# 56 small products of a constant first in TensorE's program, one summing loop for keys and values in every batch, and a new written order

## The chip, the cores and the metric

The kernel runs on one core of a Trainium2 chip. The metric is the device time of one execution in microseconds. It is measured in several runs; the comparison goes by the median. Besides, one execution is recorded by the hardware profiler, and all rows quoted here come from that one. Engines are named as the profile names them: PE (TensorE matmul), PEld (TensorE weight load), DVE (VectorE), ACT (ScalarE), POOL (GpSimd) and SP (SyncE, whose queue issues all the transfers here).

## What is computed

Attention over 32 memories per head, and behind it a feed-forward block with a spatial gate. There are 8 batches, 8 heads, 576 rows and 64 numbers per head; w_in has 512 x 1024 numbers.

```python
def _attn_ref(q, k, v, phi):
    a = phi - np.max(phi, axis=2, keepdims=True)
    a = np.exp(a)
    a = a / (np.sum(a, axis=2, keepdims=True) + 1e-09)
    k_m = np.einsum('bhsm,bhsd->bhmd', a, k)
    v_m = np.einsum('bhsm,bhsd->bhmd', a, v)
    scores = np.matmul(q, k_m.transpose(0, 1, 3, 2)) / np.sqrt(q.shape[-1])
    scores = scores - np.max(scores, axis=-1, keepdims=True)
    attn = np.exp(scores)
    attn = attn / (np.sum(attn, axis=-1, keepdims=True) + 1e-09)
    return np.matmul(attn, v_m)

def _moe_ref(x, w_in, w_spatial, b_spatial, w_out):
    h = np.maximum(x @ w_in, 0.0)
    u, v = h[..., :d_ff // 2], h[..., d_ff // 2:]
    v_n = (v - mean(v)) / np.sqrt(var(v) + 1e-06)
    v_s = np.einsum('ts,bsd->btd', w_spatial, v_n) + b_spatial[None, :, None]
    return (u * v_s) @ w_out
```

## The kernel before

Everything of a batch stays in the core's memory between loading and storing. The steps of one batch, with the letter that the written order uses for each and the names that the profile shows:

- P, `memory_weights`: load phi, take the largest value per memory over all rows (mx on VectorE; a transpose mt, a reduction cm, a broadcast cmb and a transpose back mb across the 128 partitions), subtract, exponentiate in place, and sum over rows (es).
- K, `memories`: load k and v into kv_sb, then sum phi-weighted rows with many small products of 64 partitions and 32 columns. In batches 1 to 7 one loop of 72 products takes k and v together (kvm, 128 columns wide, L411) and 8 more give the denominators (L422). Batch 0 goes another way, `first_memories`: 72 products for the keys (km, L334), the denominators (L349), scaling (den, kmn) and two transposes (tk, L373), and only later 72 products for the values (vm), vmn and tv.
- Q, `queries`: load q; batch 0 is transposed by TensorE (tq, L478, L489, L490) and copied by ScalarE (qT, L480, L494).
- S, `scores`: q times the key memories (sc). For batch 0, `first_scores` uses 64 + 16 small products (L531, L542), a softmax on VectorE and ScalarE (L560 to L579), transposes (at, L586) and the split into a high and a low part (ah, al).
- M, `products`: value memories times w_in (mp, L683), split into mh and ml. V, `gate`: pv, relu, normalisation, vh and vl. U, `units`: pu, relu, u. G, `spatial`: ps (L838), g, gh and gl. O, `project`: po (L878) and the store.

Every large product is made of three on parts of less precision (high x high, high x low, low x high).

The weights have steps of their own: D loads w_in in four pieces of 1 MB, E and L decode them (E the half that the gate uses, L the other), each in four operations: ScalarE scales (L174), GpSimd multiplies (L176), VectorE merges twice (L180, L184, the last into win_sb). W loads w_spatial, T transposes it (wt, L244; high part wth, L255; low part wtl), X does w_out, B the bias. Z is a filler: one product of the identity with itself that nobody reads (L897).

A low part can be made in two ways (`low`): VectorE subtracts, or TensorE adds minus the high part to the sum (L140) and ScalarE copies the rest (L149). The names in ON_VECTOR choose.

The order is written out by hand, in three tables: START, then PLAN once for each of batches 1 to 5, then END. A token such as S or K' runs the next part of that step, up to its next `yield`; primes mean batches ahead. Every engine works strictly through its own instructions in the order in which the tokens issue them, and SP issues transfers in that order too. A transfer into a buffer that is still being read waits on SP, with everything behind it. PSUM holds four single banks (`bank`) and two pairs (`banks`), which go round.

Of the kernel before, what the change touches and what calls it, by code (L numbers as in the profile page):

```python
# [10 lines left out]
F32 = mybir.dt.float32  # L11
# [26 lines left out]
    S' S G3 G1 G3 G0 G3 K'' G0 G1 K'' G0 G3 G0 K'' G1 S' G2*2 S'*2 O0 G2 G1 S' G3 G2 S' G3 K'''
    G1 Q'' G2 O1 G2 G3*2 S'*2 G2 S' M1' O2 P''' G3 S' O3 S' O2 S' O2 S' O0 O3 G2 V1' P''' U3' O0
    V1' P''' O4 G2 O0 O4 V0' S' K'' O3 O1 P''' O3 Q'' K'' O4 V4' O0 V0' U1' O1 V1' V0' O2 O1 M1  # L40
    V4' O4 O1 P'''
# [3 lines left out]
    U3 V1 V4 V0 K' U3 Q'*2 V4 V1 V3 V1 V4 U1 V4 U1 U2*2 V0*2 U0 U2 K' V0 V2 V4 Q' U0 V1 V3 V2  # L45
    M0' U0 M1' V3 S' V2 V4*2 V2 M0'*3 G0 M1' G0 M0' M1' V3 V2 M1'*2 V2*2 G1 G0 V3 G1 S' V3*2 G1
    S' V4 G1 G0 S'*3 G1 S' G3 G1 G3 G1 G3 G0 S'*2 U3 G0 S' G1 G2 S'*3 G1 G2 G0 S' G2 S' G0 G3 G2
    O0 S'*3 O3 S' G2 G0 V0' G2 V0' U3' V1' V0' V3' S' G3 G2 V1' V3' U2' G3 V3' G3*2 V0' V3' U2'
    O2 V4' U3' O0 U1' V0' U3' V0' U2' O0 U1' V1'*3 V4' V0' U0' V3' U0' V4'*2 O2 V4' U1' G0' U0'
    V1' G2 V4' V2' G3 V4' O1 G2 V1' V2' V4' G1' V2' V4' O2 V4' O1 G0' V3' V2' O2 V3' V2'*2 G1'  # L50
    V2' O0 O3 G0'*3 G1'*3 G3' G1' G3' G0' G2' G1' G0' G2'*2 O3 G3' G0'*2 G3' O3 G2' O3' G3'
    G1'*2 O1' G3' K' G3' O1 G2'*2 O0' O1 G2' G3' O0' O1' O3' O1' O3' O1' G2' O0' O2' O4' G3' O3'
    G2' O4'*2 O2' O0' O2' O4' O2' V0
# [9 lines left out]
def memory_attention_spatial_gate(  # L63
# [40 lines left out]

    ident = const.tile([P, P], F32, name="ident")
# [15 lines left out]
    nc.gpsimd.memset(t2[SR:P, :].bitcast(F32), 1.0)  # L121
# [151 lines left out]
    def over_rows(b, eng, to, op):  # L273
        if b == 0:
            nc.vector.tensor_reduce(to, phi_sb.rearrange("p j i m -> p j m i"), axis=AX.X, op=op)
# [3 lines left out]
        eng.tensor_tensor(half, phi_sb[:, :, 0:4], phi_sb[:, :, 4:8], op=op)
# [5 lines left out]
        eng.tensor_tensor(to, to, phi_sb[:, :, 8], op=op)  # L285
        yield

    def memory_weights(b, _):
# [7 lines left out]
        yield from over_rows(b, nc.vector, mx, ALU.max)  # L296
# [27 lines left out]
        yield from over_rows(b, engine(f"es{b}"), es, ALU.add)  # L324

    def first_memories():

        halves = (slice(0, 64), slice(64, P))

        def sums(n, to):  # L330
            for i in range(NX):
                for j in range(NJ):
                    for r in range(2):
                        nc.tensor.matmul(  # L334
                            to[r][32 * j : 32 * j + 32, 0:D],
                            phi_sb[halves[r], j, i, :],
                            kv_sb[halves[r], j, n, i * D : (i + 1) * D],
                            start=(i == 0),
                            stop=(i == NX - 1),
                        )  # L340

        km = [bank(f"km_{r}") for r in range(2)]
        sums(0, km)
        yield
        es = state.pop(("es", 0))
        esm = [x[:, D : D + 2] for x in km]
        for j in range(NJ):
            for r in range(2):
# [621 lines left out]
```

## Time and profile before

| what | value |
|---|---|
| time, median of 3 runs | 428.44 us (427.9 to 428.46) |
| the profiled execution's own time | 427.97 us |
| its span in the profile | 425.8 us |
| mean granted TensorE clock | 0.983 |
| PE busy | 404.0 us, 95% |
| DVE / ACT / POOL busy | 277.7 / 229.5 / 100.6 us |
| PE idle after 60 us, the largest groups | 3.2 us by "issue" in kvm, 2.4 us for ml |

How to read it: a row of the timeline gives start, duration, engine, source line, operation, output and inputs, partitions x elements and count; in brackets stands the idle time before it and what ended it. "Issue" means that nothing in the profile ended it. A row of the windows gives the stretch, its length and PE's busy time with the count of its products; where all engines are shown PEld, DVE, ACT and POOL follow likewise. Then come the granted TensorE clock as a share of full speed, the DMA engines' busy share, and GB/s. In a row of groups the busy time and the mean duration in ns follow the count, then the idle time before them. A row of the DMA view ends in KB and the us from issue to landing.

### The profile page before, as it was taken

Reading aid. Unit: us, or ns where it says so; the run is one execution under the profiler, and the core shown is the slowest. Engines: PE = TensorE matmul, PEld = TensorE weight load, DVE = VectorE, ACT = ScalarE, POOL = GpSimd, SP = SyncE. Lnnn points to the kernel's source line nnn. Section 1 sums busy time; section 2 is a strip of 40 time slices with the busy share of each in tenths; the row PEclk is TensorE's granted clock in tenths of the full one; section 3 lists DMA queues with packets and bytes.
Section 4 is the critical chain, followed back from the end, with each engine's and each line's share of the span. In section 5 each row is a group of like instructions: output and inputs, shape, how many; then the busy total and the mean of one; then the engine's idle time right before and its main releaser. Section 6 shows DMA issues by size and latency. Waiting matters only on the chain.

```text
span 425.8 us, 9900 instructions
## 1 busy us (share of the span) xinstructions
PE 404.0 (95%) x4179; PEld 348.8 (82%) x4179; DVE 277.7 (65%) x494; ACT 229.5 (54%) x444; POOL 100.6 (24%) x189
## 2 busy tenths in 40 slices
PE   6699899998999999999899999999999998999996
PEld 6486689786789887988698888988898877988984
DVE  3259557997888467884778377875787268944320
ACT  2438996546844287336843386337833384348312
POOL 1372574203300134012600134013401111132000
PEclk9859999999999999999999999999999999999999
DMA  8967927917580155705480157405700210000103
GB/s 308 386 267 186 241 66 225 215 37 262 138 221 3 53 183 115 167 0 181 92 219 2 74 162 184 97 26 185 112 4 0 75 50 2 0 2 25 45 32 123
DMA packets 85728, 50.73 MB, mean 119 GB/s; under 512 B 66162, under 2 KB 70258, under 8 KB 85684
## 3 DMA queue, kind: packets, MB, share of 16 engines
q1 hardware_dynamic: 85684, 50.10, 41.4%
q8 instruction: 33, 0.54, 0.6%
q14 instruction: 11, 0.09, 0.1%
HBM read 40.65 MB, written 9.44 MB: 118 GB/s over the span
## 4 chain that ended last, share of the span: by engine, by line
PE 76%; ACT 10%; DVE 7%; issue 3%; DMA 2%; POOL 1%; DVEq 0%; ACTq 0%; POOLq 0%
PE ps L838 24%; PE po L878 23%; PE pu L800 9%; PE pv L716 8%; PE kvm L411 2%; DVE ml L151 2%; PE mp L683 2%; ACT mh L692 1%; PE sc L616 1%; DMA phi_sb<-in_phi_dram 1%; PE sc L531 1%; PE wt L244 1%; ACT phi_sb L321 1%; DMA raw_out<-in_moe_w_out_dram 1%; ACT raw L174 1%
## 5 line engine op out<-in xcount | busy, mean ns | idle before, releaser
L860 ACT CAST gh<-g 128x512 fp32r<-128x512 f32 x32 | 19.8, 621 | 74.1 <-DVE g L849 74.1
L838 PE MATMUL ps<-wth,vh 128*128 128x288 f32 x256 | 56.5, 302 | 2.7 <-DVE ml L151 2.4
L838 PE MATMUL ps<-wth,vl 128*128 128x288 f32 x256 | 55.0, 296 | 0.0
L838 PE MATMUL ps<-wtl,vh 128*128 128x288 f32 x256 | 54.9, 296 | 0.0
L878 PE MATMUL po<-woh,gh 128*128 128x512 f32 x128 | 51.0, 398 | 0.0
L878 PE MATMUL po<-woh,gl 128*128 128x512 f32 x128 | 50.8, 397 | 0.0
L878 PE MATMUL po<-wol,gh 128*128 128x512 f32 x128 | 50.5, 394 | 0.0
L838 PEld LDWEIGHTS ps<-wth,vh 128*128 128x128 f32 x256 | 41.3, 188 | 6.4 <-issue 3.0
L761 DVE BATCH_NORM_STATS2 st<-vr 128x6 f32<-128x512 f32 (+1 forms) x35 | 23.8, 680 | 33.6 <-ACT vr L758 32.9
L838 PEld LDWEIGHTS ps<-wth,vl 128*128 128x128 f32 x256 | 41.2, 188 | 0.5 <-DVE vl L778 0.5
L838 PEld LDWEIGHTS ps<-wtl,vh 128*128 128x128 f32 x256 | 41.3, 188 | 0.0
L666 POOL CAST ar<-ah 128x128 fp32r<-128x128 f32 x7 | 6.1, 873 | 144.5 <-ACT ah L659 144.5
L884 ACT COPY o<-po 128x512 f32<-128x512 f32 x36 | 21.1, 585 | 33.7 <-PE po L878 22.9
L773 ACT ACTIVATE vr<-vr,few 128x512 f32<-128x512 f32 (+1 forms) x40 | 32.1, 814 | 2.1 <-POOL few L768 2.1
L849 DVE TENSOR_TENSOR g<-u,ps 128x576 f32<-128x576 f32 x32 | 24.0, 749 | 13.0 <-PE ps L838 13.0
L764 POOL TENSOR_SCALAR few<-few 128x1 f32<-128x1 f32 (+1 forms) x35 | 10.9, 310 | 88.5 <-DVE few L762 84.8
L778 DVE TENSOR_TENSOR vl<-vr,vh 128x512 fp32r<-128x512 f32 x32 | 21.6, 691 | 12.7 <-ACT vh L776 12.7
L800 PE MATMUL pu<-ah,mh 128*128 128x288 f32 x128 | 27.9, 299 | 0.9 <-ACT u L809 0.9
L878 PEld LDWEIGHTS po<-woh,gl 128*128 128x128 f32 x128 | 24.0, 188 | 5.7
L878 PEld LDWEIGHTS po<-wol,gh 128*128 128x128 f32 x128 | 24.1, 188 | 5.0
L878 PEld LDWEIGHTS po<-woh,gh 128*128 128x128 f32 x128 | 24.1, 189 | 4.6
L800 PE MATMUL pu<-ah,ml 128*128 128x288 f32 x128 | 27.4, 295 | 0.0
(194 smaller groups left out, 933.3 us busy)
## 6 DMA issues: line engine op xcount, KB each, us to landing
kv_sb<-in_k_dram SPq DMA_DIRECT2D x8, 1152.0 KB, 7.2
kv_sb<-in_v_dram SPq DMA_DIRECT2D x8, 1152.0 KB, 6.7
out_dram<-o SPq DMA_DIRECT2D x32, 256.0 KB, 2.1
q_sb<-in_q_dram SPq DMA_DIRECT2D x28, 288.0 KB, 5.7
phi_sb<-in_phi_dram SPq DMA_DIRECT2D x8, 576.0 KB, 5.1
raw<-in_moe_w_in_dram SPq DMA_DIRECT2D x4, 1024.0 KB, 17.1
raw_out<-in_moe_w_out_dram SPq DMA_DIRECT2D x4, 512.0 KB, 4.6
q_all<-in_q_dram SPq DMA_DIRECT2D x1, 1152.0 KB, 6.6
```

The source lines that it names most:

```text
L151: nc.vector.tensor_tensor(lo, x, hi.bitcast(F32), op=ALU.subtract)
L716: nc.tensor.matmul(pv, x[:, r, cs], m[:, r, DM:DFF], start=(n == 0), stop=(n == 5))
L761: nc.vector.bn_stats(st6, vr)
L764: nc.gpsimd.tensor_scalar_add(rs, mv[:, 1:2], 1e-6)
L773: nc.scalar.activation(vr, vr, AF.Identity, bias=sh, scale=rs)
L778: nc.vector.tensor_tensor(vl[:, st, :], vr, vh[:, st, :].bitcast(F32), op=ALU.subtract)
L800: nc.tensor.matmul(pu[:, hf, 0:HALF], m[:, r, cs], a[:, r, hf * HALF : (hf + 1) * HALF], start=(n == 0), stop=(n == 5),)
L838: nc.tensor.matmul(ps[:, hf, 0:HALF], a, w[:, hf * HALF : (hf + 1) * HALF], start=(n == 0), stop=(n == len(ops) - 1),)
L849: nc.vector.tensor_tensor(g.rearrange("p (a s) -> p a s", a=2), u[:, dt, :].rearrange("p (a s) -> p a s", a=2), ps[:, :, 0:HALF], op=ALU.mult,
L860: nc.scalar.copy(hi, x)
L878: nc.tensor.matmul(po, a, w, start=(n == 0), stop=(n == 11))
L884: nc.scalar.copy(o, po)
```

## The change

Four edits are made, and the three tables are written anew.

1. Ahead of everything else 56 products of a constant tile are put into TensorE's program: 64 partitions, 32 weights, 2 columns, into two PSUM banks that nobody reads. The constant is set by VectorE, so that they need not wait for the identity matrix.
2. `first_memories` is gone; batch 0 uses the same loop as the others, with k and v in one sum, so both must have landed. `over_rows` of batch 0 takes the four pairwise steps of the other batches in place of one reduction, for the maximum and for the sum.
3. The 72 products of kvm get a `yield` behind the fifth of nine rounds, so that the order may put something between them.
4. The filler Z is one product of 512 columns in place of 128, with the fp32r tile `minus`.

```diff
+    seed = const.tile([P, MEM], F32, name="seed")
+    nc.vector.memset(seed, 1.0)
+    early = [bank(f"early_{n}") for n in range(2)]
+    for n in range(56):
+        rows, at = slice(64 * (n % 2), 64 * (n % 2) + 64), 32 * (n // 2 % 4)
+        nc.tensor.matmul(
+            early[n % 2][at : at + 32, 0:2],
+            seed[rows],
+            seed[rows, 0:2],
+            start=True,
+            stop=True,
+        )
+
     ident = const.tile([P, P], F32, name="ident")
...
-    def over_rows(b, eng, to, op):
-        if b == 0:
-            nc.vector.tensor_reduce(to, phi_sb.rearrange("p j i m -> p j m i"), axis=AX.X, op=op)
-            yield
-            return
+    def over_rows(eng, to, op):
         half = one.tile([P, NJ, 4, MEM], F32, name="half")
...
-    def first_memories():
...
-        if b == 0:
-            yield from first_memories()
-            return
         kvb = [bank(f"kvm_{b}_{r}") for r in range(2)]
...
                         start=(i == 0),
                         stop=(i == NX - 1),
                     )
+            if i == NX // 2:
+                yield
         yield
...
             idle = bank("idle")
-            nc.tensor.matmul(idle[:, 0:P], ident, ident, start=True, stop=True)
+            nc.tensor.matmul(
+                idle, minus, minus[:, None, :].to_broadcast([P, NI, P]), start=True, stop=True
+            )
...
-    P*2 Z*13 P*3 Z*2 P Q P*3 K P*2 W Q*5 W D1 K D1 Q*2 D0 Z*2 K*2 Q*2 K*3 Q*2 K*3 T4 D0 T3 S X0
+    P*17 K*4 D1 K Q K E0 K*2 E0 K*2 Q K*2 Q*2 K Q E0 Q*6 W Q E0 W D0 D1 S*2 T4 D0 S Z*2 L0 S X1
```

What the tables make of the engines' programs is shown at three places. The first is the transfers that SP issues at the start; raw is w_in, w_sb and w_rem are w_spatial. Before:

```order
L290 DMA phi_sb<-in_phi_dram 128x4x288
L469 DMA q_all<-in_q_dram 128x4x576
L396 DMA kv_sb<-in_k_dram 128x4x576
L217 DMA w_sb<-in_moe_w_spatial_dram 128x4x576
L219 DMA w_rem<-in_moe_w_spatial_dram 64x576
L161 DMA raw<-in_moe_w_in_dram 128x2x1024
L396 DMA kv_sb<-in_v_dram 128x4x576
L161 DMA raw<-in_moe_w_in_dram 128x2x1024 x3
L195 DMA raw_out<-in_moe_w_out_dram 128x1024
```

And now:

```order
L299 DMA phi_sb<-in_phi_dram 128x4x288
L337 DMA kv_sb<-in_k_dram 128x4x576
L337 DMA kv_sb<-in_v_dram 128x4x576
L174 DMA raw<-in_moe_w_in_dram 128x2x1024
L409 DMA q_all<-in_q_dram 128x4x576
L230 DMA w_sb<-in_moe_w_spatial_dram 128x4x576
L232 DMA w_rem<-in_moe_w_spatial_dram 64x576
L174 DMA raw<-in_moe_w_in_dram 128x2x1024 x3
L208 DMA raw_out<-in_moe_w_out_dram 128x1024
```

q and w_spatial went behind k, v and the first piece of w_in.

The second place is the start of TensorE's program, up to the first sums. Before:

```order
L897 MATMUL idle<-ident 128x128 x13
L298 MATMUL mt_126<-ident,mx 128x128
L897 MATMUL idle<-ident 128x128 x2
L307 MATMUL mb_136<-ident,cmb 128x128
L478 MATMUL tq_153<-ident,q_all 128x128 x4
L478 MATMUL tq_159<-ident,q_all 128x128 x4
L478 MATMUL tq_165<-ident,q_all 128x128 x4
L478 MATMUL tq_177<-ident,q_all 128x128 x4
L897 MATMUL idle<-ident 128x128 x2
L334 MATMUL km_188<-kv_sb,phi_sb 32x64
```

And now, from the last two of the 56 early products on:

```order
L110 MATMUL early_75<-seed 32x2
L110 MATMUL early_76<-seed 32x2
L307 MATMUL mt_164<-ident,mx 128x128
L316 MATMUL mb_170<-ident,cmb 128x128
L349 MATMUL kvm_0_184<-kv_sb,phi_sb 32x128
L349 MATMUL kvm_1_185<-kv_sb,phi_sb 32x128
```

The 17 fillers left, and q's transposes went behind the sums, the denominators and tk. In the profile a f32 product other than a transpose stands as two products with a weight load each (the 13 fillers as 26), so the early products are 224 instructions. With them, counted as the prediction counts, the borders 194, 450, 706 and 962 fall into the early products, into kvm of batch 0 (216 instructions in, of 288), into the scores (96 in, of 256) and into the first correction of w_spatial's transposes. Further on, two borders lie in one batch's kvm and its denominators only in batch 6; in batch 5 one is in the mp just ahead of kvm and one near its end. In every batch the 72 products of kvm still stand in one row.

The third place is VectorE, from the first denominators to the softmax of batch 0. Before:

```order
L359 TENSOR_SCALAR den<-km_188 128x1
L359 TENSOR_SCALAR den<-km_189 128x1
L360 RECIPROCAL den<-den 128x2
L560 TENSOR_REDUCE rmx<-sc_0_306 128x16
L562 TENSOR_TENSOR sm<-sc_0_306,rmx 128x512
L560 TENSOR_REDUCE rmx<-sc_1_307 128x16
```

And now:

```order
L372 TENSOR_SCALAR den<-kvm_0_184 128x1
L372 TENSOR_SCALAR den<-kvm_1_185 128x1
L373 RECIPROCAL den<-den 128x2
L193 SCALAR_TENSOR_TENSOR raw<-raw 128x1024
L197 SCALAR_TENSOR_TENSOR win_sb<-raw 128x2x512
L500 TENSOR_REDUCE rmx<-sc_0_339 128x16
L502 TENSOR_TENSOR sm<-sc_0_339,rmx 128x512
```

One quarter of w_in is decoded ahead of the softmax. Inside the softmax stand two first merges, where one and a wtl stood. Behind it come the second merge that the first mp needs, the fourth first merge, a wtl, the last two second merges, and then the first ml. On ScalarE two of the four scalings of w_in now stand ahead of the first exponential of the scores, in place of one.

More of the change, by code (lines that the diff above doesn't have):

```diff
@@ L38 @@
[L38 to L41, printed above, removed]
+    M0 V0 V1 V4 U3 V0 U1 V1 P'' V2 K' V4 V0 P'' V3 P'' V1 Q' V0 V1 P'' V2 P'' Q' V4 U2*2 U1 V2
+    U0 V3 K'' U0 V3 S' P''*2 V2 S' U2 U0 M0' S'*2 M1' P''*2 V4 V2 M0' K'' M0' P'' M0'*2 M1' K''
@@ L46 @@
[L46 to L51, printed above, removed]
@@ L295, in memory_weights @@
         mx = one.tile([P, NJ, MEM], F32, name="mx")
-        yield from over_rows(b, nc.vector, mx, ALU.max)
+        yield from over_rows(nc.vector, mx, ALU.max)
         mt = bank(f"mt_{b}")[:, 0:P]
@@ L323, in memory_weights @@
         es = state["es", b] = one.tile([P, NJ, MEM], F32, tag="mx", name="es")
-        yield from over_rows(b, engine(f"es{b}"), es, ALU.add)
-    def first_memories():
[L328 to L348, printed above, removed]
-                nc.tensor.matmul(
-                    esm[r][32 * j : 32 * j + 32],
-                    es[halves[r], j, :],
-                    ones[halves[r]],
-                    start=True,
-                    stop=True,
-                )
-        yield
-        den = one.tile([P, 2], F32, name="den")
-        for r in range(2):
-            nc.vector.tensor_scalar_add(den[:, r : r + 1], esm[r][:, 0:1], 1e-9)
-        nc.vector.reciprocal(den, den)
-        yield
-        kmn = one.tile([P, 2, 2, D], F32, name="kmn")
-        for r in range(2):
-            nc.scalar.activation(
-                kmn[:, r],
-                km[r][:, None, 0:D].to_broadcast([P, 2, D]),
-                AF.Copy,
-                scale=den[:, r : r + 1],
-            )
-            yield
-        tk = bank("tk_0")[:, 0 : 2 * P]
-        for r in range(2):
-            nc.tensor.transpose(
-                tk[:, r * P : (r + 1) * P], kmn[:, r].rearrange("p c d -> p (c d)"), ident
-            )
-            yield
-        kT = state["kT", 0] = one.tile([P, 2, P], F32, name="kT")
-        nc.scalar.copy(kT.rearrange("p r s -> p (r s)"), tk)
-        yield
-        vm = [bank(f"vm_{r}") for r in range(2)]
-        sums(1, vm)
-        yield
-        vmn = one.tile([P, 2, D], F32, name="vmn")
-        for r in range(2):
-            nc.scalar.activation(vmn[:, r], vm[r][:, 0:D], AF.Copy, scale=den[:, r : r + 1])
-        yield
-        tv = bank("tv_0")[:, 0:P]
-        nc.tensor.transpose(tv, vmn.rearrange("p r d -> p (r d)"), ident)
-        yield
-        vT = state["vT", 0] = one.tile([P, P], F32, name="vT")
-        nc.scalar.copy(vT, tv)
-        yield
@@ L394, in memories @@
+        yield from over_rows(engine(f"es{b}"), es, ALU.add)
     def memories(b, _):
```

41 lines of the change are left out of this document (24 added, 17 removed).

## The prediction

> **What bounds the kernel now.** I read the page first: engines, clock, queues and the chain that ended last.
>
> ```profile
> PE 404.0 (95%) x4179; PEld 348.8 (82%) x4179; DVE 277.7 (65%) x494; ACT 229.5 (54%) x444; POOL 100.6 (24%) x189
> ...
> PEclk9859999999999999999999999999999999999999
> ...
> q8 instruction: 33, 0.54, 0.6%
> ...
> PE 76%; ACT 10%; DVE 7%; issue 3%; DMA 2%; POOL 1%; DVEq 0%; ACTq 0%; POOLq 0%
> ```
>
> TensorE is the bound over nearly the whole span, and the sum of its products hardly changes. So only three things can pay: the first 45 us, where other engines lead; waits of TensorE later on; and its clock, which is low in the second and third slice. The timeline of the first 46 us shows what happens there:
>
> ```profile
> 15.13 0.33 PE L373 MATMUL tk<-ident,kmn 128*128 128x128 f32 x1
> ...
> 19.02 0.48 PE L373 MATMUL tk<-ident,kmn 128*128 128x128 f32 x1 [3.57 <-issue]
> ...
> 19.29 1.06 PE L244 MATMUL wt<-ident,w_sb 128*128 128x128 f32 x4
> ...
> 20.29 0.37 PE L244 MATMUL wt<-ident,w_rem 64*128 64x64 f32 x1
> ...
> 20.58 3.51 PE L531 MATMUL sc<-kT,qT 64*64 64x32 f32 x121
> ...
> 25.05 0.43 PE L531 MATMUL sc<-kT,qT 64*64 64x32 f32 x7 [0.95 <-issue]
> ...
> 25.52 0.69 DVE L560 TENSOR_REDUCE rmx<-sc 128x16 f32<-128x512 f32 x1 [10.91 <-PE sc L531]
> ...
> 41.19 1.09 PE L683 MATMUL mp<-win_sb,vT 64*32 64x512 f32 x16
> ...
> 42.39 0.59 ACT L692 CAST mh<-mp 128x512 fp32r<-128x512 f32 x1 [0.30 <-PE mp L683]
> ```
>
> Two gaps of 3.57 and 0.95 us end by "issue": nothing that the profile shows released them. Between their ends TensorE ran 1 + 4 + 1 + 122 products (the scores' row shows 121; some records are missing), each with its weight load: 256 instructions. The page has 33 loads on the instruction queue for 2 x 4179 instructions, 253 a load. So TensorE waited for its own code. Counted through the program, waits included, the gaps stand at instructions 450 and 706; the borders are then 194, 450, 706, 962 and so on. Border 194 lies 41 pairs into the key sums:
>
> ```profile
> 12.32 1.66 PE L334 MATMUL km<-kv_sb,phi_sb 64*32 64x64 f32 x141
> ```
>
> That is at about 12.8 us; the code behind 450 is there at 19.02, the next at 25.05. So each block is asked for one block ahead, and takes 6.2 and 6.0 us while transfers fill the DMA engines. Windows of 2 us show the second loss:
>
> ```profile
> 18.00:20.00 2.00, 0.98 (x5) 0.93 (x5) 0.00 (x0) 0.38 (x1) 2.00 (x1) 0.65 1.06 411
> ...
> 30.00:32.00 2.00, 2.00 (x55) 1.55 (x55) 2.00 (x3) 0.00 (x0) 2.00 (x1) 0.50 0.00 0
> 32.00:34.00 2.00, 1.82 (x120) 1.54 (x107) 1.93 (x5) 0.71 (x3) 1.92 (x2) 0.94 0.03 8
> ```
>
> After the 3.57 us without products the clock (third number from the end) falls to 0.50 and stays there until about 32 us. A mean of 0.65 in the first row puts the fall at 18.6. The scores at 20.58 did not lift it.
>
> From 25.5 to 42.4 VectorE and ScalarE set the pace (softmax, decoding of w_in), then ScalarE until 57 us, then TensorE. What TensorE still waits for after 60 us is mostly this:
>
> ```profile
> PE kvm L422 <- issue: 2.5, 2, 1.4
> PE ps L838 <- DVE ml L151: 2.4, 2, 1.6
> PE kvm L411 <- issue: 0.7, 1, 0.7
> ```
>
> 3.2 us are again code: two borders inside or just ahead of 320 short instructions.
>
> **The change, part by part.** *Early products.* 56 products are 112 pairs (a f32 product is two). The nearest rows are 2 columns wide at full clock, and the score products at half:
>
> ```profile
> L349 PE MATMUL km<-ones,es 64*32 64x2 f32 x16 | 0.3, 177 | 0.0
> ...
> L531 PE MATMUL sc<-kT,qT 64*64 64x32 f32 x128 | 3.9, 291 | 1.0 <-issue 1.0
> ...
> 5.08 2.15 DVE L275 TENSOR_REDUCE mx<-phi_sb 128x128 f32<-128x1152 f32 x1 [5.08 <-DMA phi_sb<-in_phi_dram]
> ...
> 44.05 0.68 DVE L279 TENSOR_TENSOR half<-phi_sb 128x512 f32<-128x512 f32 x1
> ...
> 45.55 0.29 DVE L285 TENSOR_TENSOR mx<-mx,phi_sb 128x128 f32<-128x128 f32 x1
> ```
>
> 0.3/16 to 3.9/128 is 0.02 to 0.03 us a pair, 2.1 to 3.4 us; I take the half-clock row. They end by about 4.5 us, under phi's load (landed at 5.08), and cost nothing up to 6.9 us, when mt can start; beyond that each microsecond would count in full. They pull border 194 from 12.8 to about 4 us. At 6.2 us a load the code behind 450 is there at about 10, before the sums reach it near 13, and that behind 706 at about 19, before the scores. Both gaps go. What is late next is 962: asked for at about 22.5, there at 28.5, while TensorE reaches it near 28 with slack, as VectorE leads there. I cost it at 0; without that cover up to 1.
>
> *Loads, sums, scores.* Time to landing in the queue's order, and ScalarE's copies of q:
>
> ```profile
> q_all<-in_q_dram SPq DMA_DIRECT2D x1, 1152.0 KB, 6.6
> ...
> kv_sb<-in_k_dram SPq DMA_DIRECT2D x1, 1152.0 KB, 9.1
> ...
> w_sb<-in_moe_w_spatial_dram SPq DMA_DIRECT2D x1, 1152.0 KB, 11.8
> ...
> 10.79 2.02 ACT L480 COPY qT<-tq 128x512 f32<-128x512 f32 x4
> ...
> 15.22 0.73 ACT L494 COPY qT<-tq 64x256 f32<-64x256 f32 x2
> ...
> 258.16 2.22 PE L411 MATMUL kvm<-kv_sb,phi_sb 64*32 64x128 f32 x144
> ```
>
> Issued at 1.2, 1.8 and 2.3 us, the second to fourth places land at 7.8, 10.9 and 14.1: 3.1 us for 1152 KB. So k lands near 8, v near 10.9, the first quarter of w_in near 13.7, q near 16.8. The four-step maximum (44.05 to 45.84, 1.8 us) replaces 2.15, a gain that v's landing hides. The sums of k and v start at 11.0 and take 2.2 us at full clock, up to 3.9 at half; I take 3.3, part of each. Denominators follow at 15, kmn and vmn to 16.6, kT to 17; q's transposes and copies (2.0 + 0.7 + 0.3 for vT, behind the first transposes) run to 21.0. 128 score products at 0.0285 (3.5/122 in the timeline) end at 24.7; before, at 25.5. **Gain 0.8**; bounds -1.9 (half clock throughout: 27.4) and +2.6 (full clock: 22.9).
>
> *New order behind the scores.* VectorE from 25.4 to 42.4 us, and rows at which the stretch can be measured:
>
> ```profile
> L180 DVE SCALAR_TENSOR_TENSOR raw<-raw 128x1024 int32<-128x1024 int32 x4 | 5.1, 1273 | 0.2 <-ACT raw L174 0.2
> L184 DVE SCALAR_TENSOR_TENSOR win_sb<-raw 128x1024 int32<-128x1024 int32 x4 | 4.9, 1224 | 0.1
> ...
> L151 DVE TENSOR_TENSOR wtl<-wt,wth 128x576 fp32r<-128x576 f32 x1 | 0.7, 695 | 0.0
> ...
> 34.08 0.83 DVE L579 TENSOR_TENSOR sm<-sm,rsum 128x640 f32<-128x640 f32 x1
> ...
> 44.16 0.58 ACT L692 CAST mh<-mp 128x512 fp32r<-128x512 f32 x1 [0.85 <-DVE ml L151]
> ...
> 56.12 1.15 ACT L321 ACTIVATE phi_sb<-phi_sb 128x1152 f32<-128x1152 f32 x1
> 57.18 1.16 ACT L809 ACTIVATE u<-pu 128x576 f32<-128x576 f32 x2
> ```
>
> The softmax took 25.5 to 34.9, with one L180 and wtl in it: 9.4 - 1.3 - 0.7 = 7.4. In the changed order it holds two first merges (2.5), then one second merge (1.2); with 0.6 of waiting for the second exponential, mp can start 11.7 to 12 us behind the scores. But the second mh waits for the first ml, as it did at 44.16, and ahead of that ml VectorE now has a first merge, wtl and two second merges: 1.3 + 0.7 + 2.4 = 4.4, then 0.7 for ml. So the second mh comes about 17.0 us behind the scores, not at the 13 that mp alone would allow; before it was 44.2 - 25.5 = 18.7. That gains 1.7: one pair of merges (2.5) left for an idle VectorE, and 0.6 and some small waits come in. ScalarE is then the bound up to the first u: before 57.2 - 44.2 = 13.0; now phi's exponential (1.06 from start to start) stands behind u and work of like size on the remainder rows stands ahead, which I count at 12.2, a gain of 0.8 (0 to 1.2). Five transposes of w_spatial and a correction, 1.4 us, now stand behind mp on TensorE; its products up to the wait for u come to about 12 as well, so they hide behind ScalarE; if not, they cost up to 0.5. The fillers drop from 33 to 8 and are hidden there. **Gain 2.5** (1.0 to 3.5).
>
> *kvm in two steps, and the rest of the order.* All 72 products still stand in a row on TensorE, so the step moves nothing: 0. What moves are the borders. Batch 2's sums held two (1.1 us lost), now one, far behind the last. In batches 5 and 6 two lie 256 short instructions apart (about 2 us): 1.1 and 1.3 where 0.7 and 1.4 were lost. The waits for ml stay. **Gain 0.8** (-0.5 to 2, other waits of the new order included).
>
> Sum: 0.8 + 2.5 + 0.8 = 4.1 us. The profiled execution took 427.97 (span 425.8 and 2.2 around it), giving 423.9; it lay 0.5 under the median of 428.44, so I predict **424.3**.
>
> [...]
>
> **Rivals.**
> 1. *Half clock up to the scores.* For it: early fillers took up to 580 ns:
>
> ```profile
> L897 PE MATMUL idle<-ident x66: 275/275/580, 2.0 to 43.3; 128*128 128x128 f32 x66
> ```
>
> and narrow products did not lift the clock at 20.58. Against it: kvm fills the array as km does. Scores end at 27.4, not 24.7: 424.3 + 2.7 = 427.0. Chance 0.20. [...]
> 2. *Full clock from kvm on.* Scores end at 22.9, 1.8 earlier, and 0.7 less is lost in kvm: 421.8. Chance 0.12.
> 3. *Half clock long past the scores (the slower side).* Fillers fall from 33 to 8. In mp, pv and pu TensorE is nearly the bound, and each microsecond at half costs 0.5. From rival 1 (mp at 39.4 us, 427.0) it is slower than before once the clock returns more than 1.4/0.5 = 2.9 us later, after 42.3; at 48, 431.3. Against it: wide fillers and transposes from 28.2 to 32 lifted it before, and fillers of 512 columns stand behind the scores. Chance 0.12.
> 4. *The gaps stay*, because code is not their cause or the border only moves: 3.6 at the start and no gain in kvm, 424.3 + 3.6 + 0.8 = 428.7. Against it: the step of 256. Chance 0.10. [...]
>
> **How the numbers follow.** The forecast has 0.46, with a range of its own of 422.8 to 426.0. The range 421.2 to 428.6 leaves out rival 3, the upper part of rival 4 and the lowest of rival 2. Within 0.2% (0.9 us) is about what a measurement cannot tell from no change. Faster: 0.46 + 0.20 + 0.12 = 0.78; same 0.10; slower 0.12.
>
> **What would show it.** Right: no gap by issue before 25 us; scores ending at 24 to 25; the second mh at 41 to 42.5, waiting 2 to 3 us for ml; the first u near 54; issue waits in kvm of batches 5 and 6 only. Wrong: a gap by issue near 28 us; a clock of 0.5 beyond 33 us; a second mh later than 44; waits of ps or pv on VectorE in every batch, which would give back what the start gained.

## The result, and the profile after

| | before | changed |
|---|---|---|
| median of 20 runs each | 428.48 us (427.01 to 429.99) | 431.16 us (428.06 to 434.43) |
| the profiled execution's own time | 427.97 us | 428.06 us |
| its span | 425.8 us | 426.3 us |

The changed kernel is slower: ratio 1.0059, 95% interval 1.0035 to 1.0084. Two later series of the same kernel gave 1.0039 (1.0015 to 1.0063) and 1.0081 (1.0056 to 1.0107). A ratio leaves out executions more than 1.5% above the shortest of their kernel (three of e5, one each of e3, e11, e12 and e13), a median has them all. The forecast of 424.3 us was wrong, and so was its range up to 428.6. Note the second row: the profiled execution is the shortest of the changed kernel's 20. Its trace shows where time moved, but hardly the loss; that needed a longer execution (e16).

The page of the changed kernel, then its first 56 us (start, duration, engine, line, output and inputs, count, and the idle time before with what ended it):

```profile
PE 395.5 (93%) x4089; PEld 341.4 (80%) x4089; DVE 275.6 (65%) x501; ACT 230.2 (54%) x444; POOL 98.7 (23%) x189
...
PEclk9896999999999999999999999999999999999999
...
PE 78%; ACT 8%; DVE 4%; DMA 4%; issue 3%; POOL 1%; SPq 0%; ACTq 0%; DVEq 0%; POOLq 0%
```

```profile
0.94 1.22 PE L110 MATMUL early<-seed 64*32 64x2 f32 x112 [0.94 <-DVE seed L106]
...
6.87 0.45 PE L307 MATMUL mt<-ident,mx 128*128 128x128 f32 x1 [4.71 <-DVE mx L294]
...
11.06 3.23 PE L349 MATMUL kvm<-kv_sb,phi_sb 64*32 64x128 f32 x108 [2.55 <-DMA kv_sb<-in_v_dram]
...
17.11 0.74 PE L349 MATMUL kvm<-kv_sb,phi_sb 64*32 64x128 f32 x34 [2.82 <-issue]
...
23.57 2.07 PE L471 MATMUL sc<-kT,qT 64*64 64x32 f32 x128
...
25.69 0.69 DVE L500 TENSOR_REDUCE rmx<-sc 128x16 f32<-128x512 f32 x1 [4.69 <-PE sc L471]
...
39.17 1.09 PE L623 MATMUL mp<-win_sb,vT 64*32 64x512 f32 x16
...
42.85 0.59 ACT L632 CAST mh<-mp 128x512 fp32r<-128x512 f32 x1 [0.46 <-DVE ml L164]
...
55.06 0.64 ACT L749 ACTIVATE u<-pu 128x576 f32<-128x576 f32 x1
```

TensorE is busy for 8.5 us less than before (404.0), mainly because the fillers fell from 11.9 to 3.8 us, in a span 0.5 us longer: it stands idle more. (Of its 90 products fewer, 58 are fillers; the one summing loop saves 144 more, and the early products add 112.) The gap by issue of 3.57 us did not go. It moved forward, into the sums of batch 0, and is 2.82 us: 108 products, which are 216 instructions, ran from 11.06, and the rest at 17.11. So the softmax begins at 25.69, where 25.52 stood before. Behind it this execution gained: the first u comes at 55.06 instead of 57.18.

The clock, in windows of 3.4 us (duration, then busy time of PE, PEld, DVE, ACT and POOL with counts, granted clock, DMA share, GB/s):

```profile
25.35:28.75 3.40, 2.74 (x61) 1.87 (x54) 2.95 (x6) 1.15 (x2) 3.32 (x2) 1.00 1.03 407
28.75:32.15 3.40, 2.22 (x11) 1.26 (x11) 3.33 (x5) 3.04 (x5) 3.32 (x2) 1.00 1.05 378
32.15:35.55 3.40, 2.93 (x13) 2.46 (x13) 3.33 (x6) 2.99 (x5) 1.52 (x1) 0.50 1.05 391
35.55:38.95 3.40, 3.40 (x12) 2.40 (x10) 3.40 (x5) 2.26 (x5) 0.00 (x0) 0.50 1.11 341
38.95:42.35 3.40, 2.31 (x20) 0.66 (x19) 3.07 (x4) 2.67 (x5) 0.00 (x0) 0.99 0.63 106
```

From 32.15 to 38.95 TensorE has half its clock (0.50), and is busy all the time in the second of these windows (3.40 of 3.40 us): there it holds mp up. A window with 2.31 us busy, the last one shown, was not followed by half clock (1.00 from 39.0 to 55 us). Before the change the clock was 1.00 again from 32.25 us on. TensorE's waits behind 60 us (engine, line, released by: total, times, longest):

```profile
PE ps L778 <- DVE ml L164: 2.8, 3, 1.1
PE kvm L362 <- issue: 2.4, 1, 2.4
PE mt L307 <- DVE mx L294: 2.0, 1, 2.0
PE kvm L349 <- issue: 1.0, 2, 0.5
```

The wait for code did not shrink (3.4 us; it was 3.2), and one is new: mt of batch 2, 2.0 us. It now stands ahead of products of batch 1, while phi of batch 2 lands only at 69.8.

### The profile page after: what moved, and what is told of

The parts are those of the page before. It is cut to its first block, busy times and chain, and to the rows that moved or that the text cites. A ratio compares the mean times of both kernels' runs of the same rounds, so it can differ in the third digit from the quotient of the medians.

```text
span 426.3 us, 9745 instructions
## 1 busy us (share of the span) xinstructions
PE 395.5 (93%) x4089; PEld 341.4 (80%) x4089; DVE 275.6 (65%) x501; ACT 230.2 (54%) x444; POOL 98.7 (23%) x189
## 4 chain that ended last, share of the span: by engine, by line
PE 78%; ACT 8%; DVE 4%; DMA 4%; issue 3%; POOL 1%; SPq 0%; ACTq 0%; DVEq 0%; POOLq 0%
PE ps L778 27%; PE po L818 23%; PE pv L656 7%; PE pu L740 7%; PE kvm L349 3%; PE mp L623 2%; DMA kv_sb<-in_v_dram 2%; DMA phi_sb<-in_phi_dram 2%; ACT vr L713 1%; PE wt L257 1%; DVE ml L164 1%; PE sc L556 1%; PE pv L664 1%; ACT mh L632 1%; PE pv L672 1%
## 5 line engine op out<-in xcount | busy, mean ns | idle before, releaser
L704 POOL TENSOR_SCALAR few<-few 128x1 f32<-128x1 f32 (+1 forms) x35 | 8.7, 250 | 100.1 <-DVE few L702 99.0
L698 ACT ACTIVATE vr<-pv 128x512 f32<-128x512 f32 x28 | 16.8, 600 | 25.3 <-PE pv L656 23.2
L164 DVE TENSOR_TENSOR ml<-mp,mh 128x512 fp32r<-128x512 f32 x28 | 18.7, 687 | 14.2 <-ACT mh L632 14.2
```

Of the source, the lines that this page charges most:

```text
L164: nc.vector.tensor_tensor(lo, x, hi.bitcast(F32), op=ALU.subtract)
L698: nc.scalar.activation(vr, pv, AF.Relu)
```

## Experiments

Each kernel was timed beside the kernel before on the same chip; ratios are to that, with 95% intervals. "Code behind 450" is the block of TensorE's program that begins with instruction 450, as in the prediction.

### Where does the code come from, and when? (e2 to e5, e13)

Four counts of early products, and the 56 alone in the kernel before.

```diff
-    for n in range(56):
+    for n in range(120):     # e3; 60 in e5, 58 in e13, none in e2
```

```diff
 # e4: before.py, with the early block of the change and nothing else
+    seed = const.tile([P, MEM], F32, name="seed")
+    nc.vector.memset(seed, 1.0)
+    early = [bank(f"early_{n}") for n in range(2)]
...
     ident = const.tile([P, P], F32, name="ident")
```

> The changed kernel without the 56 early products; all else as it is. The borders of TensorE's code move 224 instructions later in its program: 194 into the sums of batch 0, 450 into its scores. Theory E (the early products bring nothing, since the block is not there earlier for being asked for earlier): a gap by issue still stands near 17 to 19 us or later, scores end within 0.7 us of 25.6, median 430.5 to 432. Theory P (as in the prediction, the early products pull the asking forward): without them the scores end 1.5 us or more later than 25.6, median 433 or more. Rival C (moving the borders of the later batches is what costs, through the wait of 2.4 us in batch 6's sums): the start is as in P or E, but after 60 us TensorE waits 2 us less, median 428 to 429.5.

> 120 early products instead of 56, so that instruction 450 is the first product of the 113th, reached at about 3.4 us: it measures directly when the block behind 450 comes if it is asked for at the border 194 (about 1.9 us). Theory Q (it is asked for there and then waits behind the transfers that were issued up to then): the early products stop near 3.4 us and go on only at 15 to 17 us; mt begins after 15, median 437 or more. Theory N (the block is asked for only a certain number of instructions ahead of its use, and takes about 6 us when the transfers fill the DMA engines): they go on near 8 to 9 us, mt is 1 to 2 us late, median 431 to 434. Theory I (a load asked for this early is quick): a gap under 1 us, mt at 6.9, no gap by issue in the sums of batch 0; then scores end near 23 us and the median is 428 to 430.

> The kernel before with the 56 early products alone added (and the column of ones they read); order, sums and fillers as before. Prediction's theory: both gaps by issue (3.57 and 0.95 us) go and scores end 3 to 4 us earlier, second mh near 42.5, median 425 to 427. Theory E (the load is not earlier for being asked for earlier): a gap of 2 to 4 us remains, now 224 instructions earlier in the program, in the key sums, ending near 17 us; scores end at 24 to 26 us; median 427.5 to 429.5.

| | products | median | ratio |
|---|---|---|---|
| e2 | 0 | 434.94 | 1.0145 (1.0107 to 1.0183) |
| e3 | 120 | 432.27 | 1.0079 (1.0052 to 1.0105) |
| e4 | 56, order of before | 430.22 | 1.0032 (1.0014 to 1.0050) |

TensorE in e3:

```profile
0.94 2.19 PE L110 MATMUL early<-seed 64*32 64x2 f32 x223 [0.94 <-DVE seed L106]
...
8.51 0.32 PE L110 MATMUL early<-seed 64*32 64x2 f32 x17 [5.38 <-issue]
...
12.75 3.23 PE L349 MATMUL kvm<-kv_sb,phi_sb 64*32 64x128 f32 x108 [2.33 <-DMA kv_sb<-in_v_dram]
...
18.84 0.74 PE L349 MATMUL kvm<-kv_sb,phi_sb 64*32 64x128 f32 x34 [2.86 <-issue]
```

The border 450 is where the count puts it, among the early products: they stop at 3.13 and go on at 8.51. If the block was asked for at the border, at about 2 us, it came by 8.5, as the prediction had it, and theory N's time fits. But the second gap tells more. The next border again lies 216 instructions into the sums, and its code comes 6.09 us after the first sum (18.84 - 12.75). In the changed kernel that was 6.05 (17.11 - 11.06). In e3 TensorE had passed the border before it at 8.51, 10.3 us earlier; in the change at about 1.9, 15 us earlier. By these two rows the time does not run from the border. They fit a start where TensorE stood waiting: at the first sum, 40 instructions behind it (194 + 40 is 234, 450 + 40 is 490).

In e2 the sums ran without a gap, the scores ended near 23, and 3.81 us by issue came behind them: theory P had the median but not the way, and E neither. In e4 two gaps stayed (2.23 and 2.52 us, both in the scores, the last of which ended at 26.5, before at 26.3), and a third of 0.73 us stood in the value sums; the prediction's theory fell there, and E had the gap in the wrong place.

If 40 is not enough, a few products more should be:

> 60 early products instead of 56: each border of TensorE's code comes 16 instructions earlier in the work. In the traces so far a block lands some 6 us after TensorE has passed a place about 40 instructions behind the border before it; with 56 that place (194 + 40) is the very first product of kvm of batch 0, which waits for v until 11.06 us. Theory 40: with 60 the place is passed among the early products, so the block behind 450 is there near 8 us; the sums run without the gap of 2.82 us (144 products in about 4.1 us, ending at 15.2), scores end at 22.5 to 23.2 instead of 25.6. Then the border 962 is reached at 23, its code comes at about 27: a gap by issue of 3 to 4 us behind the scores, clock 0.5 after it, and the median is 432 to 436, as without early products (434.9). Rival V (the block waits behind v in the queue, whatever the place): the gap in the sums stays and ends near 17.1; scores end at 25.6, median 430 to 431.5.

> The changed kernel with 58 early products instead of 56 and nothing else. Theory 40 (the block behind 450 is asked for when TensorE has passed a place 41 to 48 instructions behind 194; with 56 the sums that wait for v stand at instruction 40 behind it, with 58 at 48): no gap in the sums of batch 0, scores end at 22.7 to 25 us, median 426.5 to 429, some 3 us under the change. Rival (60 gave 431.2 in e5, so the early place is not what made e11 fast, but the order of the rest and mt): median 430.5 to 431.5.

TensorE in e13 (58):

```profile
11.15 4.07 PE L349 MATMUL kvm<-kv_sb,phi_sb 64*32 64x128 f32 x140 [2.56 <-DMA kv_sb<-in_v_dram]
...
22.09 2.07 PE L471 MATMUL sc<-kT,qT 64*64 64x32 f32 x128
...
28.48 0.38 PE L257 MATMUL wt<-ident,w_sb 128*128 128x128 f32 x2 [0.67 <-issue]
```

Two more products, 8 instructions, and the gap is gone; 0.67 us are left behind the scores. e13 has a median of 428.16, ratio 1.0006 (0.9982 to 1.0030), which is 0.3 to 0.8% under the three series of the change; its interval meets that of the mildest of these alone, e1. With 60 (e5) the gap is gone as well, and the gap behind the scores was 1.03 us and not 3 to 4. Its profiled execution took 425.49 us, but its median was 431.19, ratio 1.0037 (1.0009 to 1.0066), under the range of theory 40 and no better than the change; it and e13 differ by 0.3% in the ratio, with intervals that overlap. So both traces show the gap gone, but what that is worth in the median is not settled by them. What scatters a kernel such as e5 from 425.5 to 433.6 is the subject of the third part.

The DMA view dates the block itself by its packet on the instruction queue (q8):

| | products | packet of the block behind 450 | TensorE ran on last before it, with |
|---|---|---|---|
| changed | 56 | 14.69 | the first sums, 11.06 |
| e13 | 58 | 11.74 | mb, 8.12 |
| e5 | 60 | 10.58 | mt, 6.98 |
| e3 | 120 | 6.09 | early products, up to 3.13 |

At the eleven gaps of the first 33 us in the traces of before, the change, e2, e3, e4, e5 and e13, TensorE goes on 2.3 to 2.6 us behind a packet. In the first three rows the packet comes 3.6 us behind the moment at which TensorE runs on after a wait, and 3.6 + 2.4 is the 6.05 us found above. So theory 40 is right about the gap, but not about its reason: 58 products do not bring the packet among the early products, at about 2 us, but forward by one wait, from 14.69 to 11.74. By that the code is there at about 14.2 (an estimate, 2.3 to 2.6 us behind 11.74), just as the sums reach it. The three places lie 40, about 45 and about 50 instructions behind the border, so no one fixed place fits them all; what sets off the request stays open.

### Which half of the new order costs? (e7, e8)

```diff
 # e7: after.py with the other two tables; e8: before.py with the changed two
-PLAN = ...changed...   END = ...changed...
+PLAN = ...before...    END = ...before...     # one K more where the sums are
 # e8 besides:
+            if i == NX // 2:
+                yield
```

> The changed kernel up to batch 1, with the order of the kernel before for the rest (the sums in two steps kept, one behind the other). Borders of code stay where the change has them, within one instruction: two in the sums of batch 6, 0 wait in batches 2 and 4. Theory B (what costs behind 60 us is where the borders fall, and the waits of batch 2's mt): a gap of 1.5 to 2.5 us by issue in batch 6, mt of batch 2 waits 1.4 to 2.0 us, median 430 to 431.5 with the same wide scatter. Theory O (the new order of the later batches costs): median 428 to 429.

> The kernel before up to batch 1, with the changed order for the rest and the sums in two steps, one behind the other. Borders of code stay where the kernel before has them: gaps by issue in the sums of batches 2 and 5 (1.1 and 1.4 us), none in 6. Theory B: median within 0.7 us of the kernel before, and its narrow scatter (2 us). Theory O: 1.5 to 3 us slower than the kernel before, in waits of ps for ml.

| START | PLAN and END | ratio |
|---|---|---|
| changed | before (e7) | 1.0019 (1.0003 to 1.0035) |
| before | changed (e8) | 1.0046 (1.0030 to 1.0061) |
| changed | changed | 1.0059 (1.0035 to 1.0084) |

Theory O holds: the borders of code stand where they stood, and yet the new order of the later batches alone costs 0.46%, 2.0 us; the new START costs 0.19%, 0.8 us. Together that is 0.65%, where the three series of the change show 0.59, 0.39 and 0.81. TensorE's waits behind 60 us in e8 say on what:

```profile
PE kvm L423 <- issue: 3.3, 2, 1.9
PE ps L839 <- DVE ml L150: 3.2, 4, 1.1
PE kvm L410 <- issue: 1.0, 2, 0.8
PE mp L684 <- ACT u L810: 0.7, 1, 0.7
```

Against the rows of before (2.5, 2.4, 0.7 and 0.3) that is 2.3 us more: 1.1 for code, at borders that have not moved, 0.8 for ml, 0.4 for u. It is spread over several places; none of them was tried alone.

### Why do executions of the changed kernel differ by 6 us? (e1, e16, e6, e9)

> The changed kernel, unaltered, for a second trace and more times. Its 20 runs so far spread from 428.06 to 434.43 us (the one profile at hand is of the fastest, 428.06), the kernel before from 427.0 to 430.0. Theory S (the start decides: the wait for the code behind instruction 450 and the clock state after it differ from execution to execution): a profiled execution of 430 us or more is later by its excess already when the first u begins (55.06 us in the trace at hand), and from there to the end the two traces agree within 0.5 us. Theory O (the new order decides, not the start): the first u stands within 0.5 us of 55.06, and the excess comes later, in waits of TensorE. Median expected 431, ratio 1.004 to 1.008, by both.

> The changed kernel unaltered, for a trace of one of its longer executions (two traces so far are of its fastest, 428.06 and 427.87). Theory W: a profiled execution of 430 us or more shows one or more further windows of 3.4 us at half clock, behind the wait of batch 2's mt (73 us), behind the gap in batch 6 (262 us) or before the first u, each costing up to 1.7 us, and these make up most of the excess. Rival: no further window; the excess lies in waits for DMA or other engines. Median 430 to 431.5.

e1 profiled another short execution (427.87 us; median 430.08); e16 one of 432.19 (median 431.64). Its rows beside those of the first trace, the sums of batches 1 and 2. First the trace shown above, then e16:

```profile
60.50 2.25 PE L349 MATMUL kvm<-kv_sb,phi_sb 64*32 64x128 f32 x144
...
94.79 2.25 PE L349 MATMUL kvm<-kv_sb,phi_sb 64*32 64x128 f32 x144
```

```profile
63.01 2.25 PE L349 MATMUL kvm<-kv_sb,phi_sb 64*32 64x128 f32 x144
...
98.80 2.25 PE L349 MATMUL kvm<-kv_sb,phi_sb 64*32 64x128 f32 x144
```

The spans differ by 4.1 us: 2.5 up to batch 1's sums, 1.5 from there to batch 2's, 0.1 in all the rest. Of the 2.5, 1.4 arise between the first tk and the scores, which took 5.9 us against 4.5. This too is half clock, by the durations: in e16 each of q's last transposes, shortly ahead of the scores, takes 0.42 us up to 25.4, in the first trace 0.27. In e13 they take 0.42 where the granted clock is 0.50, up to 21.5 us, and 0.27 behind that, where it is 1.00. The 1.5 stand here, in e16's TensorE and its windows of 2 us:

```profile
76.00 0.30 PE L307 MATMUL mt<-ident,mx 128*128 128x128 f32 x1 [1.97 <-DVE mx L294]
...
77.50 0.69 PE L778 MATMUL ps<-wtl,vh 128*128 128x288 f32 x2
...
80.59 0.42 PE L778 MATMUL ps<-wth,vl 128*128 128x288 f32 x2
```

```profile
74.00:76.00 2.00, 0.03 (x1) 0.03 (x1) 1.97 (x6) 0.31 (x1) 0.00 (x0) 1.00 0.90 249
76.00:78.00 2.00, 2.00 (x12) 2.00 (x13) 2.00 (x5) 1.51 (x5) 0.00 (x0) 0.71 1.07 195
78.00:80.00 2.00, 2.00 (x10) 2.00 (x10) 1.11 (x2) 1.11 (x3) 1.68 (x1) 0.50 0.98 157
```

Batch 2's mt waits 1.97 us, and then a pair of products takes 0.69 us for about 3.4 us, at half clock (0.50 in the last row), before it is 0.42 again. In the short execution mt waited 1.99, and no such window followed. So the same wait cost 2 us in one execution and 3.5 in the other (1.97 + 1.5). Theory W is shown for this window; theories S and O of e1 each had a part of it, since the start and a later place both add.

A second long execution is at hand in e14 (431.34 us), whose program is the changed kernel's up to batch 5. There the loss stands behind the scores:

```profile
26.96 0.69 DVE L509 TENSOR_REDUCE rmx<-sc 128x16 f32<-128x512 f32 x1 [5.29 <-PE sc L480]
...
49.47 0.63 PE L681 MATMUL pv<-ml,ah 128*64 128x512 f32 x1
...
59.08 0.64 ACT L758 ACTIVATE u<-pu 128x576 f32<-128x576 f32 x1
```

In the first trace, at 1.00, that product of pv takes 0.39 us. From the start of the softmax to the first u it is 32.1 us here, against 29.4 in the first trace, 29.5 in e1 and 29.6 in e16. The granted clock was 0.50 from 36 to 40 us and again from 46 to 50. Batch 2's mt cost nothing extra in e14. So each execution loses at other places: e16 at the start and behind mt, e14 behind the scores.

Over all 38 runs, the 11 with a mean granted clock of 0.989 or more have a median of 428.6, the other 27 of 431.3. That mean leaves out the start, where the clock is not recorded (see e6 below).

How the clock might be kept full, at the start (e6) and behind the scores (e9):

```diff
 # e6: 54 early products, and
-    P*17 K*4 D1 K Q K E0 ...
+    Z*8 P*17 Z*4 K*4 D1 K Q K E0 ...
```

```diff
 # e9: 8 fillers more, at four places ahead of waits for ScalarE
-    ... E1 S T1 S W T1 Z ... T4 T3 S*2 ... S Z M1 S*2 M1 S P' B M1*2 ...
+    ... E1 S Z*2 T1 S W T1 Z ... T4 Z*2 T3 S*2 ... S Z*3 M1 S*2 M1 S P' B Z*2 M1*2 ...
```

> The borders as with 60 early products, but 8 fillers of 512 columns ahead of mt and 4 more between mb and the sums (54 early products, so that the count is the same). [...]

> The changed kernel with 8 more fillers of 512 columns, two each ahead of the products that wait for ScalarE at 30.5, 32.6, 42.4 and 43.5 us; borders behind them come 16 instructions earlier in the work. Theory W (a window of 3.4 us of which TensorE leaves about a third idle is followed by one at half clock, the windows lie differently in every execution, and that makes the change's scatter and most of its loss): the dips behind 28 us are gone or half as long, mp starts at 36.5 to 38 us instead of 39.2, granted clock 0.985 or more in most runs, median 428 to 429.5, fewer runs above 432. Rival (the scatter comes from elsewhere, as ScalarE and VectorE lead there anyway): mp at 39 or later, median 430 to 431.5, spread as before.

e6's first products:

```profile
2.47 3.78 PE L837 MATMUL idle<-minus 128*128 128x512 f32 x8 [0.35 <-ACT minus L127]
6.92 0.45 PE L307 MATMUL mt<-ident,mx 128*128 128x128 f32 x1 [0.67 <-DVE mx L294]
...
11.11 3.60 PE L349 MATMUL kvm<-kv_sb,phi_sb 64*32 64x128 f32 x144 [0.85 <-DMA kv_sb<-in_v_dram]
```

And mt in the kernel before, behind 26 fillers of 128 columns:

```profile
7.37 0.30 PE L298 MATMUL mt<-ident,mx 128*128 128x128 f32 x1 [0.81 <-DVE mx L275]
```

In e6 mt still takes 0.45 us. Its 144 sums take 3.60, 25 ns each, where the first 108 of the changed kernel take 30 and those of later batches 15.6. The median is 430.22, that of e5 431.19. So twelve fillers did not bring mt and the sums to the durations of full clock. That the changed kernel starts at half clock is read from durations (mt at 0.45 us for 0.30, q's transposes in e16), although the views say 1.00 there. They say so for want of a record: the trace's record of the clock begins at 15.11 us in the first trace and at 25.64 in e16, where the transposes become fast, and what is not recorded counts as 1.00.

e9 met its numbers: mp at 37.66, median 429.46, ratio 1.0020 (1.0002 to 1.0039), no run above 431.4, clock 0.986 or more in all runs. The eight fillers take back half of the loss or more, though the interval meets that of the mildest series of the change. That they do so by the clock alone is not shown: they also move all later borders by 16 instructions (waits for code behind 60 us: 2.1 us in e9's trace; 3.4, 1.7 and 2.4 in three traces of the change), and the longest run of e9, 431.39, has a clock of 0.995.

### One wait, and the causes together (e10, e11, e12)

All three have the changed START and the rest of the order as before (e7). e10 moves one token, e11 adds two early products, e12 adds e9's fillers.

```diff
-    ... G2 Q'' P'' G3 G0*2 P'' G1 ...
+    ... G2 Q'' G3 G0*2 P''*2 G1 ...
```

> As e7 (changed start, order of the rest as before the change), and batch 2's mt stands 18 products of 288 columns later in TensorE's program; nothing else. Theory: the wait of 1.4 to 2.0 us is gone, and with it the half-clock window that it starts in some executions (78 to 82 us in e6's trace): median 426 to 427.3 against e7's 428.7. Rival (the wait only moves, to mb or to the sums of batch 2 behind it): median 428 to 429.

> As e10, with 58 early products: borders 8 instructions earlier in the work, so that the place where the next block is asked for is passed among the early products. Theory 40: no gap by issue in the sums of batch 0, scores end near 23, a gap by issue of 1 to 3 us behind them; in executions without further dips 3 us earlier than e10 all through. Median 424 to 427; lowest run 422 to 424. Rival (what the start gains, the clock gives back: the gap behind the scores puts TensorE at half clock until mp): median as e10's within 0.7 us.

> As e11, with the 8 fillers of e9. If the clock gives back the start's gain (theory W), the fillers keep it: median 1 to 2.5 us under e11's, 422.5 to 425, spread under 4 us. If not, as e11 within 0.7 us.

| | median | ratio |
|---|---|---|
| e10 | 428.88 | 1.0013 (0.9993 to 1.0033) |
| e11 | 426.68 | 0.9933 (0.9905 to 0.9961) |
| e12 | 425.04 | 0.9921 (0.9894 to 0.9947) |

In e10 mt waits no more, but the product behind it does:

```profile
74.41 0.54 PE L777 MATMUL ps<-wth,vh 128*128 128x288 f32 x2 [0.83 <-DVE g L788]
```

So the rival held there: TensorE comes to where VectorE has not yet emptied the bank. e11 against e10 is the two early products alone: 0.8% by the ratios, 2.2 us by the medians (7 and 12 runs). e12 is the fastest kernel of this study, 0.8% under the kernel before; against e11 its fillers tell little, as the intervals overlap.

### The border in batch 6 (e14, e15)

```diff
 # e14: {5: 27, 6: 22}; e15: {5: 21, 6: 22}, with 58 early products and e9's fillers
+        for n in range({5: 27, 6: 22}.get(b, 0)):
+            r = n % 2
+            nc.tensor.matmul(kvb[r][0:32, 200:202], seed[halves[r]], seed[halves[r], 0:2], ...)
         yield
         den = one.tile([P, 2], F32, name="den")
```

> The changed kernel with 27 products of 2 columns more behind the denominators of batch 5 and 22 behind those of batch 6 (written to unused columns, about 0.02 us each, 0.5 us a batch): the borders of code in the sums of batch 6 move from 47 and 303 instructions behind their start to 195 alone, in batch 7 to 194. Theory B (in the later batches it is the border's place that costs): the gap of 1.7 to 2.4 us in batch 6 is gone, no gap by issue in batches 6 and 7, TensorE's run from the sums of batch 5 to the end 0.8 to 1.5 us shorter, fewer executions with a half-clock window behind it; median 428.5 to 429.8. Rival (the gap covers waits for ml that come then instead): unchanged, 430 to 431.5.

> The changed kernel, its order untouched, with 58 early products, the 8 fillers of e9, and small products behind the denominators of batches 5 and 6 (21 and 22) that keep two borders out of the sums of batches 6 and 7. If the three causes (place of the request, clock behind the scores, border in batch 6) add up: 431 - 3 - 1.3 - 1.3 = 425.4; 424.5 to 427. If the new order of the later batches costs besides (1.7 us, by e7 and e8), it stays 1.5 to 2 us above e12's 425.0: 426.5 to 427.5.

e14: 429.44, ratio 1.0025 (1.0003 to 1.0048), and in the sums of batch 6:

```profile
261.74 1.58 PE L349 MATMUL kvm<-kv_sb,phi_sb 64*32 64x128 f32 x97 [0.86 <-issue]
263.81 0.82 PE L349 MATMUL kvm<-kv_sb,phi_sb 64*32 64x128 f32 x40 [0.48 <-issue]
```

The gap is halved (1.3 for 2.4), not gone, and the added products take up what it gives: from batch 5's sums to the end 217.3 us as in the first trace. Theory B is not shown for batch 6. e15 came to 427.66, ratio 0.9983 (0.9964 to 1.0002), above what three adding causes would give and a little above what was expected with the order's cost. Its shifted borders opened a new gap in batch 3, 2.55 us, and behind that one stands a window of half clock (granted 0.57 from 118 to 122 us):

```profile
117.56 0.19 PE L362 MATMUL kvm<-ones,es 64*32 64x2 f32 x1 [2.55 <-issue]
...
119.18 0.69 PE L787 MATMUL ps<-wtl,vh 128*128 128x288 f32 x2
...
122.23 0.43 PE L787 MATMUL ps<-wth,vl 128*128 128x288 f32 x2
```

## Why the prediction was wrong, by its own steps

**The step that failed first** is in the early products: "They pull border 194 from 12.8 to about 4 us. At 6.2 us a load the code behind 450 is there at about 10". The border was pulled to about 1.9, better than forecast, and the code was there at 17.1 and not at 10. Its packet came at 14.69, not at the border but further on: with 56 products TensorE stands 40 instructions behind the border and waits for v until 11.06; from there to the code it is 6.05 us. At the first gap of before the two could not be told apart, as TensorE ran through 40 instructions within half a microsecond. At the second they could: border 706's code, counted from 40 instructions behind 450 (an estimate from the rows, 21.0), took 4.1 us there and not 6.0, so even from there the time was not the same at both gaps. With 58 products the gap goes (e13, e11), with the code there at about 14.2 by the estimate above. Of the two gaps that were to go, the second, 706, did. Rival 4 said that the gaps stay, for another reason.

**Early products, own cost**: 1.22 us, under phi's load: right, and cheaper than the 2.1 to 3.4 taken.

**Scores at 24.7**: 25.6. The sums ran at half clock by their durations, 30 ns a product for 15.6 in later batches, where the prediction took a mean; the gap of 2.82 us did the rest. With the gap gone the 128 products end at 24.2 in e13 and 22.6 in e5, ahead of the forecast.

**Order behind the scores, 2.5**: right in sum. From the softmax's start to the first u it is 29.4 to 29.6 us in three traces of the change (forecast 29.2; before 31.7), though not in e14 (32.1). That both parts match in the first trace is luck: the second mh stands 17.2 us behind the softmax's start (forecast 17.0) and the first u 12.2 behind it (12.2), but in e1 and e16 it is 15.9, and 13.5 and 13.7. The reason given, a wait of 2 to 3 us for ml, was 0.46; mp was late, held up at half clock (0.50) from 32 to 39. In e9 four transposes of at shortly ahead of mp took 0.60 us, for 1.06 to 1.11 at half clock in e14; mp came at 37.66, and there the second mh did wait 1.68 for ml.

**Half clock**: rival 3 had it past the scores, with fillers cut from 33 to 8, but as one stretch with a fixed end. In the traces it came in windows that lie differently in each execution (0.50 from 32.15 to 38.95 in the first, from 36 to 40 and 46 to 50 in e14, from 78 to 80 in e16), and the loss is in the median (428.6 at a mean clock of 0.989 or more, 431.3 below), with the shortest executions free of it. e9 (429.46) lies some 1.5 us under the median of all 38 runs of the change (431.0); how much of that is the clock, and how much the borders that its fillers move, is not shown. In the traces, half clock behind the scores cost 2.5 us or more in e14 and next to nothing up to the first u in the others, estimated from the 32.1 us for 29.4 to 29.6 above.

**Rest of the order, +0.8**: -2.0 (e8). Costed at nothing, kvm in two steps was right, its products stand in one row. The borders in batches 5 and 6 were forecast at 1.1 and 1.3 us; 0.5 and 2.4 were seen. The waits for ml did not stay but grew (2.8 to 4.5 us for 2.4). mt of batch 2 stands in no term of the sum: the new START places it ahead of work that could have covered phi's transfer, and it waits 1.2 to 2.0 us. By e10 moving it alone gains nothing, as TensorE then waits for g.

So the sum of +4.1 became -2.7: the START's +3.3 became -0.8 (e7), the rest's +0.8 became -2.0 (e8). With 58 products and the old order behind it, the START's part measures +2.9 by the ratio and +1.6 by the medians (e11). Open: which moves in PLAN and END cost the 2.0, why two executions of one kernel place the windows differently, what sets off the request for the next block, and whether 60 early products (e5) are truly worse than 58 (e13): 3 us by the medians, 0.3% by ratios that overlap.

## What to carry to other kernels

Where an engine waits for its own code, date the load by its packet on the instruction queue, and see what the engine was waiting for some 4 us ahead of it (3.6 here): eight instructions moved that packet by 3 us (14.69 to 11.74) and decided over a gap of 2.8. Before fillers are taken out, look for stretches of some 3.4 us in which the engine would be a third idle (half clock stood here behind one with 2.22 us busy), and take several traces: one trace, above all of a short execution, doesn't show what the median pays. An order that is better at one place moves waits and borders at all later ones; swap the parts of the order singly.

## What the hardware showed that was not expected

- The packet of the next block of TensorE's code was not tied to the border of 256 instructions: in the changed kernel, e13 and e5 it came at 14.69, 11.74 and 10.58 us, each 3.6 us behind the end of a wait some 40 to 50 instructions past the border, and TensorE went on 2.3 to 2.6 us behind a packet at the gaps of the start. Together that took 6.05 us in the changed kernel, and 6.09 at the second gap of e3, with the transfers of the start in flight. A border met early cost 5.38 us in e3. What sets off the request is not known; the runs only bracket it.
- The clock fell to half behind a window in which TensorE was busy 2.22 of 3.40 us (first trace), and behind a single wait of 1.97 us (e16), though not behind one of 1.99 (first trace). It did not fall behind a window with 2.31 us busy. It stayed at 0.50 for about 3.4 us in e16, 6.8 in the first trace (32.15 to 38.95) and 13.7 in the kernel before (18.6 to 32.25). By these rows two thirds busy was too little once, and enough once. At the start mt took 0.45 us, in the kernel before 0.30.
- The clock that the views show is 1.00 where the trace has no record of it: ahead of 15.11 us in the changed kernel's first trace and of 25.64 in e16, while products there take up to twice their time (30 ns a sum for 15.6). It is to be read together with durations.
- A wait of 1.97 us on TensorE cost 3.5 in e16, by the window behind it; in e15 such a window stands behind a gap of 2.55.
